# Weight splits held back while row maxima are due, and stages of the attention shifted, in a kernel whose instruction order is written out by a planner

## The chip, the cores and the metric

The kernel runs on one core of one Trainium2 chip. The metric is the device time of one execution in microseconds (us). Before the change the median of three runs is 1079.9 us (1079.01 to 1081.43).

## The reference, cut to what matters

One input X (2048 positions, width 640, fp32) goes through two blocks whose results are mixed by a gate.

```python
q, k, v = x @ wq, x @ wk, x @ wv          # 32 heads of 20, 4 segments of 512 positions
for s in range(4):
    p = softmax(qs @ ks.T * scale + mask)  # causal, inside the segment
    a_dot = p @ vs
    a_mem = (phi(qs) @ M) / (phi(qs) @ z + 1e-6)   # memory of the segments before
    o_s = g_h * a_mem + (1 - g_h) * a_dot
    M, z = M + phi(ks).T @ vs, z + sum(phi(ks))
a = o @ wo
b = (silu(x @ w1) * (x @ w3)) @ w2         # SwiGLU, inner width 1728
out = gate * a + (1 - gate) * b            # gate = sigmoid(sum(x * gate_w))
```

## The kernel before, in words

Every large matmul works on weights and activations that are split into a high and a low part, in three passes, and on halves of 64 rows, so that two matmuls can run side by side in TensorE (PE). A weight tile is loaded by a DMA (line 494), its high part is cast on ACT (line 181), and its low part is a subtraction on POOL (line 176, tile W). Letters in the profile are tiles: q, k, v, g, u, f and op are products with weights; s are logits, t transposed logits, P their exponentials, o the product of P with V; nd, gm, gd, gt and rr belong to the memory term and to the division by the row sums.

The attention runs over 64 pairs of heads (16 pairs for each of the 4 segments), and two pairs make a quad. For a pair, `s_unit` makes logits in three parts (s..._0 to s..._2) and DVE takes the row maxima from PSUM (line 1161, a custom instruction and a read of its result). `max_rows` splits the maxima of a quad, `turn` transposes them on DVE (line 1187), and `row_in` sends them by four small DMAs of POOL's queue (line 1171, qk<-mr, two for each pair) into two more rows of the pair's tile of q and k. `t_unit` then makes the transposed logits with the maximum already subtracted; its matmuls (line 1212) wait for these DMAs. ACT exponentiates (line 1219), POOL masks (line 1228), and `pv_quad` multiplies with V (line 1245). `load_pair` fetches q and k of a pair with two DMAs of 240 KB in the same POOL queue (line 1126, qk<-qkd). At the end of a segment, `o_sums` reads the row sums back, `o_scale` inverts them on DVE (line 1309) and scales them (line 1310).

The order on every engine is written out in Python. The planner keeps a clock for each engine and walks through slots: 40 slots (n) for a quad (m). The tables S_AT and T_AT put the units into slots, `after(k, f)` files f into the list `soon`, and `tick` counts k down by one at every slot. Between the units, steps of the other jobs are laid in at a fixed spacing: `w_step` runs once every STEP = 700 ns of planned time and splits the oldest loaded weight tile when its age allows it, and `braid(a, b, every, skip)` puts steps of job b between those of job a at a spacing `every` (ns of planned time) after a lead of `skip`. Each engine takes its instructions strictly in the order written, so one that waits holds everything behind it on that engine. PSUM has eight banks, handed out in turn: a matmul into a bank waits until the reader of the bank's last contents is done.

Of the kernel before, what the change touches and what calls it, by code (L numbers as in the profile page):

```python
# [21 lines left out]
S, D, H, DH, NSEG, L = 2048, 640, 32, 20, 4, 512  # L22
# [19 lines left out]
COL, COL4, MIN_MM, APART, ISSUE, AHEAD = 0.4533, 1.7, 62, 5, 580, 500  # L42
STEP, READ = 700, 222
EVAC = 1500
LAND, SPARE, NOP = 4200, 99999, 80
ENGINES = ("PE", "SP", "Activation", "DVE", "Pool")

# [2 lines left out]
def gated_mix(ctx: ExitStack, tc: tile.TileContext, xT, wqk, wv, w13, w2, w2h, wo, beta, out):  # L50
# [71 lines left out]
    def here(ins):  # L122
        return ins
# [9 lines left out]
    def now():  # L133
        return max(clocks)
# [315 lines left out]
    def room(tag, n=1):  # L450
        return sum(t <= now() for t in rings[tag]) >= n
# [8 lines left out]
    def big_tile(name, dt=F32):  # L460
        return sp.tile([P, KB * L], dt, tag="big", name=name, bufs=1)
# [16 lines left out]
    def limit():  # L478
        return NW + clock["oldest"] - sum(h < clock["oldest"] for s in floors.values() for h in s)

    early, raws, clock = [], [], dict(slot=0, step=0, oldest=0, next=0, raws=2)
# [33 lines left out]
    def w_step():  # L515

        clock["step"] += 1
        if raws and raws[0][0] in EARLY:
            if clock["step"] >= 6 + 2 * raws[0][0]:
                w_split()  # L520
        elif raws and raws[0][0] < limit() and now() >= raws[0][3]:
            w_split()
        use = clock["raws"] - NRAW
        if clock["next"] < min(len(items), limit() + NRAW) and \
                (use < 0 or use < len(freed) and now() >= freed[use]):
            w_load()
# [90 lines left out]
    def load_raw(c):  # L617

        wide = big_tile(f"xr{c}")
        xraw[c] = [wide[:, kb * L:(kb + 1) * L] for kb in range(KB)]  # L620
        for kb in range(KB):
            store_later(xraw[c][kb], xT[c, :, kb, :], ("x", c, kb))
        return
        yield
# [326 lines left out]
    def job_read(c):  # L951
        return 5.6, memory_read(c)
# [101 lines left out]
    def ffn_down(cs, js, idx, last=False, free=None):  # L1054
        first = js[0] == 0
        def tile_of(c, lb, hf):
# [18 lines left out]
            def evac(ps, bank):  # L1075
                dst = accs[c][:, lb, 320 * hf:320 * hf + 320]
                if first:
                    until[bank] = go("act", 530)
                    nc.scalar.activation(dst, ps[:, :320], AF.Copy, scale=cgate[:, c, lb:lb + 1])
                elif NF in js and busy["dve"] > max(busy["act"], now()) + EVAC and busy["pool"] < now() + 600 and room("f", 3):  # L1080
                    name = f"fe{c}_{lb}_{hf}"
# [33 lines left out]
    oall, heads, pairs = {}, {}, {}  # L1115
# [60 lines left out]
    def max_rows(p):  # L1176

        flush(lambda: all(f is not s_unit or q > p + 1 for _, f, q, _ in units))
        while min(pairs[p + k].get("rows", 0) for k in range(2)) < 6:
            force()  # L1180
        m = pairs[p]["m"]
        ns = nsT[p // 2 % 2]

        def turn():
            mr = sp.tile([32, P], F32, tag="mr", name="mr", bufs=1)
            for g in range(4):
                nc.vector.transpose(mr[:, 32 * g:32 * g + 32], ns[32 * g:32 * g + 32].bitcast(F32))
            go("dve", 840)
            for k in range(2):
                for a in range(2):  # L1190
                    dst = pairs[p + k]["t"][RH + a:RH + a + 65:64, 0].rearrange("h (b n) -> h b n", n=P)
                    r = 16 * a + 8 * k
                    after(3 + 6 * k + a, row_in, pairs[p + k], dst, mr[r:r + 8])

        split_psum(ns.rearrange("p (a n) -> p a n", a=2), m, f"nh{p}", turn, 200)

# [67 lines left out]
    def o_sums(c):  # L1264
        sums_of[c] = t = f_tile(f"rs{c}", "dve")
        here(nc.sync.dma_start(t[:, :P], od[c][:, DH].rearrange("h (a n) -> h a n", n=P)))
        go("sp", 600)
        after(9 if c < NSEG - 1 else 5, o_scale, c)
        after(4 if c < NSEG - 1 else 2, o_load, c, KB - 1)

    def o_load(c, b):
# [106 lines left out]
    soon = []  # L1378

    def after(n, f, *a):  # L1380
        soon.append([n, f, a])
# [8 lines left out]
    NQUAD = NJ // 4  # L1390
# [15 lines left out]
    def attention():  # L1406


        for m in range(-1, NQUAD + 2):
            for n in range(40):  # L1410
                if m == -1 and n < 40 - LEAD:
                    continue
                clock["slot"] += 1
                if n == 3 and 0 <= m - 2 < NQUAD:
                    units.append((clock["slot"], pv_quad, 2 * m - 4, 0))
                if n in S_AT and 0 <= m < NQUAD:
                    i, x = S_AT[n]
                    units.append((clock["slot"], s_unit, 2 * m + i, x))
                if n in T_AT and 0 <= m - 1 < NQUAD:
                    i, x = T_AT[n]  # L1420
                    units.append((clock["slot"], t_unit, 2 * m - 2 + i, x))
                if n == 24 and 0 <= m < NQUAD:
                    after(9, max_rows, 2 * m)
                if n in ((22, 32) if m < 0 else (28, 39)) and m + 1 < NQUAD:
                    p = 2 * (m + 1) + (n > 28)
                    flush(lambda: all(q % NST != p % NST for _, _, q, _ in units))
                    load_pair(p)
                if units and (units[0][0] + 2 * LATE < clock["slot"]):
                    unit()
                tick()  # L1430
                yield m
# [113 lines left out]
    def down_with_out(cs, g, c, mid):  # L1545

        plan = plan_wo()
        floors["o", c] = held = set(plan)
        o1, o2 = oproj(c, plan, held)
        cost, f = job_down(cs, g)  # L1550

        def mix():
            yield from islice(o2, 4)
            yield from islice(f, mid)
            yield from o2
            yield from f

        return (3.5, o1), (17.8 + cost, mix())
# [19 lines left out]
    def job_down(cs, g, last=False):  # L1578
        return 2.384 * sum(3 if j < NF else 1.5 for j in GROUPS[g]), ffn_down(cs, GROUPS[g], plan_down(GROUPS[g]), last)

    def jobs_up(cs, g):
        return [job_up(cs, j) for j in GROUPS[g]]

    def jobs_group(cs, g):
        return [job_up(cs, j) for j in GROUPS[g]] + [job_down(cs, g)]
# [14 lines left out]
    def alternate(a, b):  # L1600

        def gen():
            for y in a[1]:
                yield y
                z = next(b[1], None)
                if z is not None:
                    yield z
            yield from b[1]
        return a[0] + b[0], gen()

    def take(a, n):
        return a[0] / 2, (y for _, y in zip(range(n), a[1]))

    def chain(jobs):
        return sum(c for c, _ in jobs), (y for _, g in jobs for y in g)

    def braid(a, b, every, skip=0, rest=True):

        def gen():
            side = Side(b[1], every, skip)  # L1620
            yield side
            yield from a[1]
            side.on = False
            if side.held is not None:
                yield side.held
            if rest:
                yield from b[1]
        return a[0] + b[0], gen()

    A, B = (0, 1), (2, 3)  # L1630
# [7 lines left out]
    k, warm = bank_tile("warm")  # L1638
    until[k] = 8000.0
    for n in range(9):  # L1640
# [5 lines left out]

    seg = job_q2(A, 3)
    g = jobs_group(A, 0)
    seg += [braid(chain(g[:3]), job_read(1), 3800, 11000)] + g[3:] + jobs_group(A, 1) + jobs_up(A, 2) + [job_down(A, 2)]
    segs.append((H + LAG + 3, seg))  # L1650
    u = jobs_up(A, 5)
    o1, ud = down_with_out(A, 5, 0, 3)
    seg = [braid(chain(u), o1, 1400, 4000), ud]
    u0, u1 = jobs_up_by_chunk(A, 6)
    xs = chain([(0, new_x(2)), (0, new_x(3))])
    d0, d1 = jobs_down_by_chunk(A, 6)
    out0 = (0, store(0))
    q2, v2 = chain(job_q2((2,), 0, {2: big_tile})), job_v((2,))[0]
    seg += [(0, load_raw(2))] + u0 + [braid(braid(chain(u1), xs, 2700, 3400, False), d0, 900, 1000, False)]
    seg += [braid(braid(chain([d0, take(q2, 2), d1, q2, v2]), out0, 700), xs, 3000, 4000)]  # L1660
    seg += jobs_k(B)
    segs.append((2 * H + 4, seg))
    seg = job_q((2,), 2)
    q = job_q2(B, 3, {3: slot}) + job_q2((3,), 0) + job_q((3,), 2)
    up = job_up(B, 0)
    r = job_read(2)
# [3 lines left out]
    o1, ud = down_with_out(B, 0, 1, 1)  # L1670
    seg = [braid(braid(chain(main), chain([r, job_read(3)]), 1800, 0), o1, 1500, 5000),
           braid(ud, (0, store(1)), 900), *jobs_up(B, 1), job_down(B, 1)]
    segs.append((3 * H + LAG + 4, seg))
    u = jobs_up(B, 2)
    o1, ud = down_with_out(B, 2, 2, 4)
    seg = [braid(chain(u), o1, 1800, 2000), ud, *jobs_up(B, 3)]
    d = job_down(B, 3)
    seg.append(take(d, 7))
    segs.append((NJ + LAG + 0, seg))
    u = [job_up(B, j) for j in GROUPS[4]]  # L1680
    d2, d3 = jobs_down_by_chunk(B, 4)
    o1, o2 = jobs_oproj(3)
    tail = [braid(chain([d] + u + [d2, take(d3, 6)]), o1, 1100, 7000), alternate(take(o2, 3), take(d3, 0)), o2, d3]

    def at_job(n):
        if n == 0:
# [24 lines left out]
    while run:  # L1711
# [10 lines left out]
        while credit > 0:  # L1722
            d = step(run[1])
# [59 lines left out]
```

## Time and profile before

| | |
|---|---|
| median of 3 runs | 1079.9 us |
| profiled execution | 1081.12 us |
| its span on the core | 1079.3 us |
| granted TensorE clock | 1.000 of full speed |
| PE busy / weight loads (PEld) busy | 1072.3 us (99%) / 974.8 us (90%) |
| DVE / ACT / POOL busy | 577.7 / 490.4 / 572.0 us |
| chain that ended last | PE 96%, DMA 2%, POOL 1% |

The span is what the profiler sees between the first and the last instruction; the 1.8 us around it belong to start and end. Busy time of the engines other than PE matters only where PE waits for them. In the timeline a row is a run of like instructions (x2 is two of them), and the words in brackets give the idle time of that engine just before the row and what ended it.

### The profile page before, as it was taken

How to read it: one execution, taken by the hardware profiler on the slowest of the kernel's cores; microseconds unless marked ns; L12 is line 12 of the kernel's file. 1: busy time of each engine (PE TensorE's matmuls, PEld its weight loads, DVE VectorE, ACT ScalarE, POOL GpSimd, SP SyncE). 2: the span in 40 equal slices, each digit the busy share in tenths (PEclk: the TensorE clock that was granted, in tenths of full speed). 3: DMA queues.
4: the chain of work that ended last, by engine and by line, in shares of the span. 5: the costliest groups of instructions: out<-in, count | busy, mean ns of one | idle time of the engine just before them, and what ended most of it. 6: DMA issues, size and time to landing. Idle time of an engine off the chain costs nothing.

```text
span 1079.3 us, 29722 instructions
## 1 busy us (share of the span) xinstructions
PE 1072.3 (99%) x11681; PEld 974.8 (90%) x11681; DVE 577.7 (54%) x1740; ACT 490.4 (45%) x1015; POOL 572.0 (53%) x767
## 2 busy tenths in 40 slices
PE   9999999999999999999999999999999999999998
PEld 7999998978888999999988889999989889988998
DVE  6022565355545666656444766763446665553464
ACT  6255434644344344365656654445442444344221
POOL 3543456376366463546665556655554774574341
PEclk9999999999999999999999999999999999999999
DMA  9365754344353332528587876454444453442231
GB/s 323 129 207 193 265 142 124 77 109 113 80 133 105 101 88 68 172 68 260 162 279 221 281 230 196 138 148 113 129 116 99 124 141 78 105 130 66 62 99 74
DMA packets 88099, 154.98 MB, mean 144 GB/s; under 512 B 19628, under 2 KB 34904, under 8 KB 87960
## 3 DMA queue, kind: packets, MB, share of 16 engines
q1 hardware_dynamic: 56520, 96.88, 28.7%
q0 software_dynamic: 23664, 42.04, 15.9%
q10 hardware_dynamic: 7776, 14.16, 3.6%
q8 instruction: 93, 1.52, 0.6%
q14 instruction: 46, 0.38, 0.1%
HBM read 97.55 MB, written 54.53 MB: 141 GB/s over the span
## 4 chain that ended last, share of the span: by engine, by line
PE 96%; DMA 2%; POOL 1%; issue 0%; ACT 0%; SPq 0%; DVE 0%; POOLq 0%
PE g L266 19%; PE f L266 17%; PE u L266 17%; PE op L266 7%; PE v L266 7%; PE o L1245 6%; PE k L266 6%; PE q L266 4%; PE t L1212 4%; PE s L1150 4%; DMA qk<-mr 1%; PE pm L266 1%; PE q L778 1%; PE nd L266 1%; PE pkt L264 0%
## 5 line engine op out<-in xcount | busy, mean ns | idle before, releaser
L266 PE MATMUL g<-X,W 64*128 64x512 f32 x1680 | 398.9, 396 | 0.0
L266 PE MATMUL u<-X,W 64*128 64x512 f32 x1560 | 375.2, 394 | 0.0
L1161 DVE CUSTOM_DVE_ANT_0 junk<-s,mask 128x128 bf16<-128x128 f32 (+3 forms) x512 | 250.9, 490 | 165.4 <-PE s L1150 127.6
L266 PEld LDWEIGHTS g<-X,W 64*128 64x128 f32 x1680 | 276.6, 185 | 12.7 <-issue 1.8
L176 POOL TENSOR_TENSOR W<-wr,W 128x640 fp32r<-128x640 f32 (+1 forms) x132 | 206.6, 1572 | 145.2 <-ACT W L181 135.2
L266 PE MATMUL f<-W,ht 64*128 64x320 f32 x2592 | 276.1, 308 | 0.0
L266 PEld LDWEIGHTS u<-X,W 64*128 64x128 f32 x1560 | 259.5, 185 | 12.1 <-issue 1.2
L266 PEld LDWEIGHTS f<-W,ht 64*128 64x128 f32 x2592 | 260.5, 185 | 2.4 <-issue 1.6
L1219 ACT ACTIVATE P<-t 128x384 f32<-128x384 f32 (+1 forms) x384 | 180.4, 525 | 174.1 <-PE t L1212 158.4
L1228 POOL TENSOR_SCALAR_AFFINE_SELECT P<-P 128x256 f32<-128x256 f32 (+1 forms) x192 | 93.4, 495 | 172.3 <-ACT P L1219 165.0
L181 ACT CAST W<-wr 128x640 fp32r<-128x640 f32 (+1 forms) x138 | 98.4, 727 | 34.1 <-PE f L266 15.7
L266 PE MATMUL op<-W,oT 64*128 64x320 f32 x960 | 103.9, 307 | 0.0
L266 PEld LDWEIGHTS op<-W,oT 64*128 64x128 f32 x960 | 98.9, 185 | 0.9 <-issue 0.6
L266 PE MATMUL k<-X,W 64*128 64x512 f32 x600 | 98.2, 400 | 0.0
L1212 PE MATMUL t<-qk 62*128 62x256 f32 (+2 forms) x512 | 95.0, 326 | 1.7 <-DMA qk<-mr 1.7
L1026 POOL TENSOR_TENSOR ht<-ft,ht 128x512 fp32r<-128x512 f32 x52 | 67.2, 1293 | 52.3 <-ACT ht L1033 47.6
L1095 DVE SCALAR_TENSOR_TENSOR acc<-f,cgate,acc 128x320 f32<-128x320 f32 x124 | 66.6, 547 | 49.2 <-PE f L266 46.9
L1150 PE MATMUL s<-qk 60*128 60x256 f32 (+2 forms) x512 | 92.2, 325 | 0.0
L266 PE MATMUL v<-W,X 64*128 64x322 f32 (+2 forms) x948 | 90.6, 310 | 0.0
L1126 POOL DMA_DIRECT2D qk<-qkd x128 | 69.6, 548 | 35.1 <-PE f L266 29.9
L266 PEld LDWEIGHTS v<-W,X 64*128 64x128 f32 (+1 forms) x948 | 86.3, 186 | 0.3 <-ACT phi_qs L706 0.2
L266 PE MATMUL q<-X,W 64*128 64x512 f32 x480 | 83.7, 396 | 0.0
(121 smaller groups left out, 1312.4 us busy)
## 6 DMA issues: line engine op xcount, KB each, us to landing
qk<-qkd POOLq DMA_DIRECT2D x128, 240.0 KB, 4.2
wr<-in_w_dram SPq DMA_DIRECT2D x80, 320.0 KB
qkd<-qs SPq DMA_DIRECT2D x20, 512.0 KB
qkd<-ks SPq DMA_DIRECT2D x20, 512.0 KB
od<-oq ACTq DMA_DIRECT2D x32, 256.0 KB
wr<-in_wo_dram SPq DMA_DIRECT2D x20, 320.0 KB
vg<-vd SPq DMA_DIRECT2D x16, 336.0 KB
qkd<-qs SPq DMA_DIRECT2D x20, 256.0 KB
```

Source lines behind the costliest of these rows:

```text
L176: return lambda: e.tensor_sub(dst[:, 1], src, dst[:, 0].bitcast(F32))
L181: stages(bank, ("act", ns, lambda: nc.scalar.copy(dst[:, 0], src)), low, done=done)
L266: ins = nc.tensor.matmul(o, l, x, start=i == 0 and (r == 0 or not w.todo[0]), stop=i == len(todo) - 1 and (r == 1 or not w.todo[1]), skip_ ...
L1026: nc.gpsimd.tensor_sub(ht[:, 1], t, ht[:, 0].bitcast(F32))
L1095: nc.vector.scalar_tensor_tensor(dst, ps[:, :320], cgate[:, c, lb:lb + 1], dst, op0=ALU.mult, op1=ALU.add)
L1126: here(nc.gpsimd.dma_start(t[64 * i:64 * i + RH], qkd[c][RH * (h + i):RH * (h + i + 1)]))
L1150: nc.tensor.matmul(ps[i][:, o:o + n], q[:, qb * P:(qb + 1) * P], k[:, :n], start=qb != 1, stop=qb != 0, skip_group_check=True)
L1161: nc.vector.tensor_tensor_reduce(out=junk[:, :n], in0=ps[i][:, o:o + n], in1=mask[:, L - n:], scale=1.0, scalar=-3.0e38, op0=ALU.add, op1= ...
L1212: nc.tensor.matmul(ps[i][:, o:o + L - q0], k[:, kb * P:(kb + 1) * P], q[:, q0:], start=kb != 2, stop=kb != 3, skip_group_check=True)
L1219: nc.scalar.activation(u["P"][:, i, o:o + n], ps[i][:, b:b + n], AF.Exp, scale=SCALE)
L1228: nc.gpsimd.affine_select(d, d, pattern=[[0, 2], [0, n], [1, P]], base=0, channel_multiplier=-1, compare_op=ALU.is_ge, fill=0.0)
L1245: nc.tensor.matmul(ps[32 * i:32 * i + 32, kb * P:], heads[2 * p + i]["v"][:, kb], pairs[p + i // 2]["P"][:, i % 2, o:o + n], start=kb == 0 ...
```

## The change: what it does

A constant HOLD = 4 is added. `w_step` no longer begins to split a weight tile while a `row_in` stands in `soon` with fewer than 4 slots to go; the first tiles (EARLY) are not held. The `row_in` of a quad's second pair move from 9 and 10 slots after the transposition to 11 and 12. `o_scale` comes after 8 slots and not 9, in segments 0 to 2. `pv_quad` is filed at slot 2 of a quad and not at 3. Eight numbers in the lists of jobs change: six spacings and leads of `braid`, and two counts of steps (the last argument of `down_with_out`, and a `take`).

```diff
+HOLD = 4
...
-        elif raws and raws[0][0] < limit() and now() >= raws[0][3]:
+        elif raws and raws[0][0] < limit() and now() >= raws[0][3] and not any(f is row_in and n < HOLD for n, f, _ in soon):
             w_split()
...
-                    after(3 + 6 * k + a, row_in, pairs[p + k], dst, mr[r:r + 8])
+                    after(3 + 8 * k + a, row_in, pairs[p + k], dst, mr[r:r + 8])
...
-        after(9 if c < NSEG - 1 else 5, o_scale, c)
+        after(8 if c < NSEG - 1 else 5, o_scale, c)
...
-                if n == 3 and 0 <= m - 2 < NQUAD:
+                if n == 2 and 0 <= m - 2 < NQUAD:
                     units.append((clock["slot"], pv_quad, 2 * m - 4, 0))
...
-    seg += [braid(chain(g[:3]), job_read(1), 3800, 11000)] + g[3:] + jobs_group(A, 1) + jobs_up(A, 2) + [job_down(A, 2)]
+    seg += [braid(chain(g[:3]), job_read(1), 3600, 11000)] + g[3:] + jobs_group(A, 1) + jobs_up(A, 2) + [job_down(A, 2)]
...
-    tail = [braid(chain([d] + u + [d2, take(d3, 6)]), o1, 1100, 7000), alternate(take(o2, 3), take(d3, 0)), o2, d3]
+    tail = [braid(chain([d] + u + [d2, take(d3, 6)]), o1, 1100, 9000), alternate(take(o2, 2), take(d3, 0)), o2, d3]
```

The two programs hold the same instructions in the same numbers; only their order differs, and up to pair 16 the order on PE is the same. Line numbers of the changed kernel are higher by one. Three places follow, with the row after a kernel's name being the order on one engine.

First DVE, at the end of segment 0 (near 359 us of the trace before): the logits s19_1 of pair 19 and the inversion of the row sums rs0. Before:

```order
L1161 ISA junk_5610,m36_5217<-s19_1_0_5605,mask_85 128x384
L1161 ISA m36_5217 128x1
L1161 ISA junk_5612,m36_5217<-s19_1_1_5606,mask_85 128x384
L1161 ISA m36_5217 128x1
L1309 RECIPROCAL rs0_5521<-rs0_5521 128x128
L1095 SCALAR_TENSOR_TENSOR acc1_2960<-f1_6_0_0_5506,cgate_99,acc1_2960 128x320
```

and in the changed kernel:

```order
L1310 RECIPROCAL rs0_5514<-rs0_5514 128x128
L1162 ISA junk_5609,m36_5218<-s19_1_0_5604,mask_85 128x384
L1162 ISA m36_5218 128x1
L1162 ISA junk_5611,m36_5218<-s19_1_1_5605,mask_85 128x384
L1162 ISA m36_5218 128x1
L1096 SCALAR_TENSOR_TENSOR acc1_2960<-f1_6_0_0_5510,cgate_99,acc1_2960 128x320
```

The inversion (RECIPROCAL rs0) has moved ahead of the two row maxima (ISA junk, each with the read of its result) of s19_1, behind which it stood.

Second ACT, in segment 2 (near 666 us): t37 are transposed logits of pair 37, v3_2_1 is a product for V of segment 3, vv3_2_1 its copy in SBUF, vd3 the store of it. Before:

```order
L1219 ACTIVATE P37_10700<-t37_1_0_10770 128x384 [waits PE_49]
L1219 ACTIVATE P37_10700<-t37_1_1_10771 128x384 [waits PE_49]
L860 COPY vv3_2_1_10795<-v3_2_1_10606 128x16x20 [waits DMAHW7_49,PE_49]
L866 ACTIVATE gate_98<-v3_2_1_10606 128x1
L1219 ACTIVATE P37_10700<-t37_2_0_10809 128x384 [waits PE_49]
L1219 ACTIVATE P37_10700<-t37_2_1_10810 128x384 [waits PE_49]
L688 DMA vd3_75<-vv3_2_1_10795 128x336 [waits Activation_49,Pool_49]
```

and in the changed kernel:

```order
L861 COPY vv3_2_1_10797<-v3_2_1_10603 128x16x20 [waits DMAHW5_49,DMAHW1_49,PE_49]
L867 ACTIVATE gate_98<-v3_2_1_10603 128x1
L1220 ACTIVATE P37_10701<-t37_1_0_10802 128x384 [waits PE_49]
L1220 ACTIVATE P37_10701<-t37_1_1_10803 128x384 [waits PE_49]
L689 DMA vd3_75<-vv3_2_1_10797 128x336 [waits DMAHW4_49,Activation_49,Pool_49]
L1220 ACTIVATE P37_10701<-t37_2_0_10826 128x384 [waits PE_49]
L1220 ACTIVATE P37_10701<-t37_2_1_10827 128x384 [waits PE_49]
```

The copy vv3_2_1 and the small activation behind it (gate) have moved ahead of the exponentials of t37_1, and the copy now waits for two other DMA semaphores (DMAHW5 and DMAHW1) than before (DMAHW7).

Third PE, some 18 us later (near 685 us): s41_0 are logits of pair 41, g3_1, u2_1 and u3_1 products of the SwiGLU block. Before:

```order
L266 MATMUL g3_1_11046<-X3_7809,W86_10092 128x512
L266 MATMUL u3_1_11099<-X3_7809,W87_10313 128x512
L266 MATMUL g3_1_11046<-X3_7809,W86_10092 128x512
L1150 MATMUL s41_0_0_11133<-qk1_87 128x256 [waits DMASW6_49,DVE_49]
L1150 MATMUL s41_0_1_11134<-qk1_87 128x256 [waits DMASW7_49,Activation_49]
L1150 MATMUL s41_0_0_11133<-qk1_87 128x256
L1150 MATMUL s41_0_1_11134<-qk1_87 128x256
```

and in the changed kernel:

```order
L267 MATMUL u2_1_10923<-X2_7354,W87_10304 128x512
L1151 MATMUL s41_0_0_11104<-qk1_87 128x256 [waits DMASW5_49,DVE_49]
L1151 MATMUL s41_0_1_11105<-qk1_87 128x256 [waits DMASW6_49,Activation_49]
L1151 MATMUL s41_0_0_11104<-qk1_87 128x256
L1151 MATMUL s41_0_1_11105<-qk1_87 128x256
L267 MATMUL u3_1_11110<-X3_7809,W87_10304 128x512 [waits Activation_49]
```

Before, s41_0 comes after ten matmuls of u3_1; now it comes ahead of the first of them, and this first one has a wait for ACT of its own. t38_1, which stands a few rows above, has moved ahead by 24 matmuls of g3_1, u2_1 and u3_1, s41_0 by 20. On ACT the exponentials of t38_1 stand, in both programs, behind four casts of oT1 and the activation ft2_1.

## Rows read from the trace of the kernel before

**Rows 1.** Waits of PE, longest first: total us, times, longest.
```profile
PE t L1212 <- DMA qk<-mr: 1.7, 2, 1.4
PE warm L1641 <- DVE zero L1637: 1.3, 1, 1.3
```

**Rows 2.** Chain that ended last, in order of time: start us, us, what.
```profile
560.17 8.19 DMA qk<-mr
...
619.49 5.16 DMA qk<-mr
```

**Rows 3.** Timeline, POOL and PE near 560: start, us, work, idle before, releaser.
```profile
559.15 1.03 POOL L1126 DMA_DIRECT2D qk<-qkd  x2
...
561.70 1.56 POOL L176 TENSOR_TENSOR W<-wr,W 128x640 fp32r<-128x640 f32 x1 [0.95 <-ACT W L181]
...
568.50 0.68 PE L1212 MATMUL t<-qk 62*128 62x512 f32 x2 [1.42 <-DMA qk<-mr]
```

**Rows 4.** Windows: stretch, length, busy of PE, PEld, DVE, ACT, POOL, clock, DMA share, GB/s.
```profile
560.00:564.00 4.00, 4.00 (x37) 2.74 (x38) 2.82 (x10) 1.76 (x4) 2.98 (x5) 1.00 0.98 338
564.00:568.00 4.00, 3.08 (x42) 1.78 (x34) 0.50 (x1) 1.71 (x3) 1.61 (x4) 1.00 0.65 170
640.00:644.00 4.00, 4.00 (x57) 4.00 (x55) 1.95 (x7) 1.31 (x3) 3.98 (x8) 1.00 0.22 65
```

**Rows 5.** Timeline, DVE and PE near 359.
```profile
358.87 0.56 DVE L1161 CUSTOM_DVE_ANT_0 junk<-s,mask 128x384 bf16<-128x384 f32 x1
...
359.36 0.95 DVE L1309 RECIPROCAL rs<-rs 128x128 f32<-128x128 f32 x1
...
359.67 0.42 PE L1212 MATMUL t<-qk 62*128 62x256 f32 x4
```

**Rows 6.** Timeline, SP, ACT and PE near 666.
```profile
664.19 0.33 SPq L688 DMA_DIRECT2D gd<-gm  x1
...
666.59 0.43 ACT L860 COPY vv<-v 128x320 f32<-128x320 f32 x1 [0.21 <-PE v L266]
666.91 0.18 ACT L866 ACTIVATE gate<-v 128x1 f32<-128x1 f32 x1
...
666.75 0.49 PE L1212 MATMUL t<-qk 62*128 62x256 f32 x4
```

**Rows 7.** Tile gd: its stores, issue to landing.
```profile
DMA to landing us min/median/max: 3.3/3.9/6.0
```

**Rows 8.** Timeline, PE, DVE and ACT between 676 and 686.
```profile
676.73 0.40 PE L264 MATMUL gt<-ident,gm 64*128 64x64 f32 x4
...
677.32 0.68 DVE L1352 TENSOR_TENSOR oall<-oall,gt 128x512 f32<-128x512 f32 x1
...
678.93 0.56 DVE L1161 CUSTOM_DVE_ANT_0 junk<-s,mask 128x384 bf16<-128x384 f32 x1
...
678.03 1.24 ACT L181 CAST oT<-oall 128x384 fp32r<-128x384 f32 x3 [0.23 <-DVE oall L1352]
680.15 0.60 ACT L999 ACTIVATE ft<-g 128x512 f32<-128x512 f32 x1 [0.88 <-PE g L266]
...
684.86 0.87 ACT L1219 ACTIVATE P<-t 128x384 f32<-128x384 f32 x2 [3.49 <-PE t L1212]
...
685.60 0.49 PE L1150 MATMUL s<-qk 60*128 60x256 f32 x4
```

**Rows 9.** Chain that ended last, ten 64x512 matmuls in a row.
```profile
691.53 1.16 PE u L266 x10
```

**Rows 10.** Timeline, DVE and POOL near 674.
```profile
673.59 3.40 DVE L875 TENSOR_SCALAR gate<-gate 128x4 f32<-128x4 f32 x1
...
671.72 3.08 POOL L176 TENSOR_TENSOR W<-wr,W 128x640 fp32r<-128x640 f32 x2
...
675.39 1.57 POOL L176 TENSOR_TENSOR W<-wr,W 128x640 fp32r<-128x640 f32 x1
```

**Rows 11.** Line 875 on DVE: count, ns min/median/max.
```profile
L875 DVE TENSOR_SCALAR gate<-gate x4: 260/292/3401, 41.2 to 673.6; 128x4 f32<-128x4 f32 x4
```

More of the change, by code (lines that the diff above doesn't have):

```diff
@@ L1648, in gated_mix @@
     g = jobs_group(A, 0)
-    seg += [braid(chain(g[:3]), job_read(1), 3800, 11000)] + g[3:] + jobs_group(A, 1) + jobs_up(A, 2) + [job_down(A, 2)]
+    seg += [braid(chain(g[:3]), job_read(1), 3600, 11000)] + g[3:] + jobs_group(A, 1) + jobs_up(A, 2) + [job_down(A, 2)]
     segs.append((H + LAG + 3, seg))
     u = jobs_up(A, 5)
-    o1, ud = down_with_out(A, 5, 0, 3)
-    seg = [braid(chain(u), o1, 1400, 4000), ud]
+    o1, ud = down_with_out(A, 5, 0, 4)
+    seg = [braid(chain(u), o1, 1400, 4500), ud]
     u0, u1 = jobs_up_by_chunk(A, 6)
@@ L1658, in gated_mix @@
     q2, v2 = chain(job_q2((2,), 0, {2: big_tile})), job_v((2,))[0]
-    seg += [(0, load_raw(2))] + u0 + [braid(braid(chain(u1), xs, 2700, 3400, False), d0, 900, 1000, False)]
-    seg += [braid(braid(chain([d0, take(q2, 2), d1, q2, v2]), out0, 700), xs, 3000, 4000)]
+    seg += [(0, load_raw(2))] + u0 + [braid(braid(chain(u1), xs, 3000, 1800, False), d0, 900, 1000, False)]
+    seg += [braid(braid(chain([d0, take(q2, 2), d1, q2, v2]), out0, 700), xs, 3000, 7000)]
     seg += jobs_k(B)
```

## The prediction

> **What bounds the kernel now.** I read the page's busy shares first: PE works 99% of the span, at the full granted clock, so only time in which PE waits, or matmuls that pack better, can be won. Next came the waits of PE. There the reader is to see two groups alone: the transposed logits t wait for the small transfers of row maxima, 1.7 us in all in two places, and the start waits 1.3 us for its first operand, which the change leaves [rows 1]. No group names a weight tile: no wait for a split is on record. Then the chain that ended last: it leaves PE for two transfers of row maxima, 8.19 us and 5.16 us long [rows 2].
>
> The timeline around the longer one shows who is ahead of whom. POOL issues two loads of a pair (240 KB each) at 559.15, the row transfer at 560.17, and begins the weight split at 561.70, behind the transfer; t starts at 568.50 after 1.42 us of idle PE [rows 3]. The windows give the reason: the DMA engines are 0.98 busy in the four microseconds in which the transfer sets out, while in a quiet stretch they are 0.22 busy [rows 4]. So what held the row maxima here was other traffic, not a weight split. The second place (619.49) has the same pattern.
>
> **The change, part by part.** The sum is made against the profiled execution, 1081.1 us, which lies 1.2 us above the median.
>
> *Held splits.* A split is a cast on ACT and 1.56 us on POOL [rows 3]; holding one moves it back by a few slots. PE never waits for a weight tile in the trace, so I cost the hold at nothing; what covers it is the stock of split tiles, and if that were too short in one place, the price is a split, 1.6 us. As for its gain: at the two places where t waits, the row transfers, the pair loads and the split stand on POOL in the same order in both programs, with the split already behind. The stall stays; four small transpositions (pkt) now stand ahead of the first waiting t and fill some of it: −0.2 us. Bounds: −1.7 (both waits gone) and 0.
>
> *Row transfers of the second pair later.* By the tables the first pair of a quad has nine slots from its transfer to its t (slot 36 to slot 45), and the second had 25 and now has 23. Both recorded waits are of first pairs, with nine slots; a second pair with over twice as many costs 0. At pair 36 a load of a pair has slipped ahead of the second of the first pair's transfers; the DMA engines are nearly idle there, 0.22 [rows 4], so 0, and a miss would cost no more than the longest wait on record, 1.42 us.
>
> *The inversion of row sums one slot earlier.* RECIPROCAL, 0.95 us, now stands ahead of two row maxima of 0.56 us each with their reads. Before, the second maximum ends at about 359.4 (start 358.87), and the next t, which needs the banks that the maxima read, starts at 359.67 [rows 5]. The inversion delays the second maximum to about 360.3; with two more matmuls ahead of it t is due at 359.8: +0.45 us. Bounds: 0 (its row sums arrive late, or the bank is another) and 0.95. In the other segments no row maximum changes sides with it.
>
> *The copy ahead of the exponentials.* The change lets the copy vv3_2_1 pass the exponentials of pair 37 on ACT. The tile that it writes was read last by a store of gd. That store is issued at 664.19 before [rows 6]; nine matmuls fewer stand ahead of its data, so about 663.5 now, and such stores take 3.3 to 6.0 us to land, 3.9 at the median [rows 7]: 667.4. Copy and gate take 0.43 and 0.18 us [rows 6]; they free the bank for t37_2 at 668.0. t37_2 ran at 666.75 [rows 6] and has eight small matmuls (some 0.6 us) more ahead: due at 667.35. That is +0.65 us; by the ends of the landing times 0 and 2.7.
>
> *Logits of pair 41 earlier.* s41_0 and the u3_1 behind it need the banks that the exponentials of t38_1 empty, and these stand on ACT behind the oT casts and ft2_1. PE's side moves ahead: 20 matmuls of 0.116 us [rows 9] are 2.3 us, so s41_0 is due at 683.3 (685.60 before). ACT's side moves back: the transposition gt1_2 has 11 large and some ten small matmuls more ahead and ends near 679.3 (676.73 plus 0.4, and 2.2). On DVE its evacuation now stands behind the row maxima that end at 679.5 before [rows 8] and some 0.5 later now: 680.0, plus 0.68, four casts at 0.41, ft at 0.60 and two exponentials, 0.87 together [rows 8], make 683.5 for the first bank and 683.9 for the second. Both ends move together when PE slips earlier. Cost: 0.2 for s41_0 and 0.3 for u3_1, +0.5 us. Bounds: 0 and 3.6 (the second rival adds 3.1).
>
> *pv_quad a slot earlier, and the spacings.* One slot less for the masks of the exponentials: PE has no recorded wait for a mask [rows 1], so 0. The spacings move steps of memory, store and SwiGLU work; what that does at named places is in the terms above, the rest is 0 with half a microsecond either way.
>
> Sum: −0.2 + 0.45 + 0.65 + 0.5 = +1.4 us, 1082.5 on the profiled execution's basis, and 1081.3 on the median's.
>
> **A rule against the trace.** In the trace a DVE instruction on 128x4 numbers takes 3.40 us at 673.59, while the other three of its line lie near 0.26 to 0.29; POOL's splits run from 671.72 to 674.80 and from 675.39 to 676.96, and DVE is released as the last one ends [rows 10, 11]. The Trainium skill, "SBUF — State Buffer", section "Who interferes with whom", says that VectorE in a two-port mode and GpSimd contend for one shared pair of ports, and that the one that comes second blocks fully until the other is done. The trace agrees: 3.40 us. By this rule a split that is held back is no delay saved but a block moved to other DVE work, which makes the second rival.
>
> **The rivals.**
> *Faster: the waits for row maxima go.* If the new spacing thins the traffic ahead of the two transfers, 1.7 us goes [rows 1] and the three new waits do not come: 1079.9 − 1.7 = 1078.2. To pass the bound of 0.2% (2.16 us, about what can be told from no change here) another 0.5 us must come from better packing of matmuls. For it: 8.19 us for 4 KB leaves much to win. Against it: the order of POOL's queue is unchanged there.
>
> *Slower: splits block DVE ahead of pair 41.* In the changed order the gate instruction stands ahead of the evacuations of gt1_4 and gt1_2 (before, of gt1_2 alone, and nothing on PE waited), and two splits run back to back on POOL near it. If it meets them at their start, DVE is held 3.40 − 0.29 = 3.1 us, gt1_2's evacuation, the casts, the exponentials and s41_0 all slip, and the time is 1081.3 + 3.1 = 1084.4. It costs from the point at which DVE is held for more than nothing, since that chain has no reserve left. Against it: the third split, which prolonged the block before, is now behind the row transfers, so the gate may find POOL between splits.
>
> *Slower: the store lands late.* With 6.0 us instead of 3.9 [rows 7], t37_2 waits 2.7 instead of 0.65: 1081.3 + 2.1 = 1083.4. For it: the pair loads and V's stores share the queues there. Against it: the median.
>
> *Nothing comes through.* The stores land at 3.3 us, the evacuations have a few tenths more than I count: 1079.9, with the row waits as before.
>
> **How the numbers follow.** The sum, +0.7 to +2.1 us: 0.33, and it is the likeliest, 1081.3. Nothing comes through: 0.25. Row waits gone and better packing: 0.13. DVE blocked: 0.14. Store late: 0.15. The 0.2% bounds around the median are 1077.7 and 1082.1; the first two cases lie inside: 0.58. The faster rival, with its packing, gives 0.13, the two slower ones 0.29. The range leaves out one in ten on each side: 1077.7 (row waits and half a microsecond of packing) to 1084.5 (DVE blocked). The forecast's own range is 1080.5 to 1082.1.
>
> **What would show it.** Right: in the waits of PE, t on row maxima still near 1.5 us, and new small waits of t on DVE near 360 us, of t on ACT near 667 and of s and u on ACT near 683; the copy vv in front of the exponentials with idle ACT before it. The gate instruction of line 876 at 0.3 us or at 3 tells the second rival. Wrong: row transfers near 560 and 619 that land in 3 us, or PE's waits no longer than before with the time changed all the same, which would mean that the matmuls themselves pack differently.

## The result: about 2 us slower, and the profile after

The changed kernel takes 1081.24 us (median of 22 runs, 1079.91 to 1081.69), the kernel before 1079.26 us (22 runs, 1078.19 to 1081.43). The ratio is 1.0015, 95% interval [1.0009, 1.0021]: a loss of 1.6 us by this ratio and of 2.0 us by the medians. It is below the 0.2% that the prediction took as no change, but the interval does not hold 1. The profiled execution of the changed kernel has a span of 1079.9 us.

The waits of PE in the changed kernel (columns as in [rows 1], of which these are the counterpart):

```profile
PE warm L1642 <- DVE zero L1638: 1.3, 1, 1.3
PE nd L267 <- SPq L270: 0.5, 1, 0.5
PE t L1213 <- ACT gate L867: 0.5, 1, 0.5
PE k L267 <- SPq L270: 0.4, 1, 0.4
PE s L1151 <- DMA qk<-qkd: 0.2, 1, 0.2
PE t L1213 <- DVE m L1162: 0.2, 1, 0.2
```

The 1.7 us of t on row maxima [rows 1] are gone, and several small waits stand in their place. Two of them were forecast by name: t on DVE and t on ACT. That of nd on SP is no mark of the change: a second profile of the kernel before has it too (below). One caution goes for all of them: this view counts only time in which both halves of PE stand still. Where one half waits and the other works on alone, the loss is larger, and is read from the starts in the timeline.

The first place, DVE and PE near 360 us, the counterpart of [rows 5]:

```profile
358.81 0.94 DVE L1310 RECIPROCAL rs<-rs 128x128 f32<-128x128 f32 x1
359.67 0.49 DVE L1162 CUSTOM_DVE_ANT_0 junk<-s,mask 128x384 bf16<-128x384 f32 x1
...
360.32 0.56 DVE L1162 CUSTOM_DVE_ANT_0 junk<-s,mask 128x384 bf16<-128x384 f32 x1
...
360.48 0.28 PE L1213 MATMUL t<-qk 62*128 62x256 f32 x1
360.94 0.50 PE L1213 MATMUL t<-qk 62*128 62x256 f32 x3 [0.18 <-DVE m L1162]
```

The inversion now runs first, the second row maximum begins at 360.32, and the second half of the logits t16_2 has to wait for it. From the first matmul's start to the last one's end it is 0.96 us (360.48 to 361.44), where the same four took 0.42 [rows 5].

The second place, ACT and PE near 666 us, the counterpart of [rows 6]:

```profile
666.58 0.43 ACT L861 COPY vv<-v 128x320 f32<-128x320 f32 x1 [3.28 <-DMA gd<-gm]
666.91 0.18 ACT L867 ACTIVATE gate<-v 128x1 f32<-128x1 f32 x1
...
666.37 0.28 PE L1213 MATMUL t<-qk 62*128 62x256 f32 x1
667.13 0.50 PE L1213 MATMUL t<-qk 62*128 62x256 f32 x3 [0.48 <-ACT gate L867]
```

ACT stands idle for 3.28 us ahead of the copy vv, which waits for the store of gd; before, the copy waited 0.21 us, for PE. In the chain that ended last (start, us, what) this store has taken the place of the row maxima of [rows 2]:

```profile
662.18 4.34 DMA gd<-gm
...
930.90 5.39 DMA qk<-qkd
```

The other transfer on it, a pair load, costs s the 0.2 us of the list above.

t37_2 runs from 666.37 to 667.63, 1.26 us where it took 0.49 [rows 6]: 0.77 us.

The third place, DVE, ACT and PE between 680 and 684 us, the counterpart of [rows 8]:

```profile
680.42 0.68 DVE L1353 TENSOR_TENSOR oall<-oall,gt 128x512 f32<-128x512 f32 x1
...
681.14 1.24 ACT L182 CAST oT<-oall 128x384 fp32r<-128x384 f32 x3 [2.66 <-DVE oall L1353]
682.28 0.58 ACT L1000 ACTIVATE ft<-g 128x512 f32<-128x512 f32 x1
682.77 0.86 ACT L1220 ACTIVATE P<-t 128x384 f32<-128x384 f32 x2
...
682.65 0.39 PE L267 MATMUL g<-X,W 64*128 64x512 f32 x1
682.88 0.92 PE L1151 MATMUL s<-qk 60*128 60x256 f32 x4
683.68 1.19 PE L267 MATMUL u<-X,W 64*128 64x512 f32 x8
```

ACT waits 2.66 us for the evacuation of gt1_2, then runs casts, ft and exponentials in one unbroken row, and s41_0 takes 0.92 us in place of 0.49 [rows 8]: its second half waits for the first of the two exponentials, and u3_1 at 683.68 for the second, which ends at 683.63.

The same in windows (columns as in [rows 4]); first the kernel before in the last place, then the changed one near 560, 666 and 682:

```profile
680.00:684.00 4.00, 4.00 (x40) 4.00 (x38) 3.73 (x12) 1.21 (x2) 2.00 (x1) 1.00 0.67 205
```

```profile
560.00:564.00 4.00, 4.00 (x43) 2.95 (x43) 2.56 (x9) 2.31 (x5) 3.00 (x5) 1.00 0.94 328
...
664.00:668.00 4.00, 3.52 (x46) 3.13 (x45) 2.31 (x9) 1.42 (x5) 0.95 (x3) 1.00 0.83 261
680.00:684.00 4.00, 3.86 (x33) 3.18 (x31) 3.61 (x11) 2.86 (x7) 0.00 (x0) 1.00 0.49 130
```

In 680 to 684 PE is idle for 0.14 us only, but it starts 33 matmuls instead of 40. The two windows do not hold the same matmuls, so the columns are the better measure: by the matmuls that start inside, 16720 before and 13568 now. The difference, 3152 columns, is that of 6.2 matmuls of 512, and at 0.116 us each [rows 9] it is worth 0.7 us, most of it lost by one half alone.

Last, POOL and PE near 560, the counterpart of [rows 3]:

```profile
559.65 1.03 POOL L1127 DMA_DIRECT2D qk<-qkd  x2
560.67 0.58 POOL L1172 DMA_DIRECT2D qk<-mr  x1
562.25 1.55 POOL L177 TENSOR_TENSOR W<-wr,W 128x640 fp32r<-128x640 f32 x1 [1.00 <-ACT W L182]
...
567.44 0.45 PE L1213 MATMUL t<-qk 62*128 62x512 f32 x2
```

The order on POOL and the DMA load (0.94 busy, 0.98 before [rows 4]) are as before, yet t at 567.44 waits for nothing: the transfer landed after 6.18 us, not 8.19 [rows 2]. Whether the change did that is a question for the experiments.

### The profile page after: what moved, and what is told of

Its sections match the earlier page's. It is cut to its first block, busy times and chain, and to the rows that moved or that the text cites. A ratio compares the mean times of both kernels' runs of the same rounds, so it can differ in the third digit from the quotient of the medians.

```text
span 1079.9 us, 29731 instructions
## 1 busy us (share of the span) xinstructions
PE 1073.0 (99%) x11681; PEld 975.5 (90%) x11681; DVE 576.0 (53%) x1740; ACT 489.2 (45%) x1015; POOL 572.6 (53%) x767
## 4 chain that ended last, share of the span: by engine, by line
PE 97%; DVE 1%; DMA 1%; ACT 0%; issue 0%; SPq 0%; POOL 0%; ACTq 0%; DVEq 0%
PE g L267 19%; PE u L267 18%; PE f L267 17%; PE op L267 7%; PE o L1246 7%; PE v L267 7%; PE k L267 6%; PE q L267 5%; PE s L1151 4%; PE t L1213 4%; PE q L779 1%; PE pm L267 1%; PE nd L267 1%; DMA qk<-qkd 0%; PE pkt L265 0%; PE gt L265 0%
```

## The experiments

The theory: the loss is the sum of the three new waits, at t16_2, t37_2 and s41_0 with u3_1. The rivals: it is the hold itself, or matmuls that pack differently; and, for the waits that went, that the hold or the later transfers removed them.

**Three edits of the changed kernel, each taking one wait away, and all three at once.** These ran on one chip, beside 33 runs of the kernel before (median 1079.76).

The inversion of segment 0 in two halves, the second behind the row maxima:

```diff
-        stages(None, ("dve", 950, lambda: nc.vector.reciprocal(rs, rs)),
+            n = 64 if c == 0 else P
+            nc.vector.reciprocal(rs[:, :n], rs[:, :n])
...
+            if c == 0:
+                nc.vector.reciprocal(rs[:, 64:], rs[:, 64:])
```

> The changed kernel, with one edit: in segment 0 the inversion of the row sums is done in two halves of 64 columns, the first where the whole one stood, the second behind the two row maxima of pair 19; every other instruction stays where it was. Theory of the three waits (the sum of the prediction): the maxima end some 0.4 us earlier, the wait of t16_2 near 360 us (0.43 us in the changed kernel's trace) falls to 0.1 or less, and the time falls by 0.4 us, from 1.0015 to about 1.0011 of the kernel before. Rival (the waits are covered: PE loses nothing by them, and the time comes from matmuls that pack differently): the wait goes, the time stays at 1.0015.

Measured: 1080.89 us, 1.0011 [1.0002, 1.0020]. In its profile the wait of t on DVE is gone; that of t on ACT is 0.7 us, where the changed kernel has 0.5.

The store that the copy vv waited for, reading another tile:

```diff
-                store_later(gd[c][:, qb, 320 * hf:320 * hf + 320], gm, ("g", c, qb, hf), t=t, done=lambda: let(name))
+                src = Xs[2][:, 0, 0, :320].bitcast(F32) if (c, qb, hf) == (2, 3, 1) else gm
+                store_later(gd[c][:, qb, 320 * hf:320 * hf + 320], src, ("g", c, qb, hf), t=t, done=lambda: let(name))
```

> The changed kernel, with one edit: one store of the memory term of segment 2 (gm2_3_1, 160 KB) takes its bytes from the tile X, with the same size, queue and place, so the ring tile is not read by it (this block of the result is left out, so the output is not the reference's). The copy vv3_2_1 on ACT no longer waits for that store to land. Theory of the three waits: t37_2 near 667 us no longer waits (0.81 us in the changed kernel's trace); the time falls by 0.8 us, from 1.0015 to 1.0008. Rival (another buffer or engine is as late, the wait is given back within the next 20 us): the wait of t37_2 goes, those of s41_0 and u3_1 grow by as much, the time stays at 1.0015.

Measured: 1080.44 us, 1.0007 [0.9999, 1.0016]. The wait of t on ACT is gone, and s41_0 still takes 0.92 us: what was won at t37_2 is not given back there. In this one profile t waits 0.6 us for row maxima in another place.

Two of the four oT casts of one block on POOL instead of ACT:

```diff
-        stages(bank, ("act", ns, lambda: nc.scalar.copy(dst[:, 0], src)), low, done=done)
+        stages(bank, ("act", ns, lambda: (cast or nc.scalar.copy)(dst[:, 0], src)), low, done=done)
...
+                  cast=nc.gpsimd.tensor_copy if c == 1 and qb == 1 else None)
```

> The changed kernel, with one edit: two of the four casts of oT1 (0.41 us each) go from ACT to POOL, at the same place of the program; ACT reaches ft2_1 and the exponentials of t38_1 some 0.8 us earlier. Theory of the three waits: s41_0 and u3_1 near 683 us wait 0.60 and 0.55 us in the changed kernel; now 0 and 0.3 at most; the time falls by 0.8 us, from 1.0015 to 1.0008. Rival (DVE's evacuation of gt1_2 or PE itself sets the end there, or POOL is late): waits as before, time at 1.0015.

Measured: 1080.51 us, 1.0007 [0.9998, 1.0016]. s41_0 takes 0.61 us (683.03 to 683.64) in place of 0.92, and u3_1 starts beside it, at 683.32.

All three edits together:

> The edits of the three kernels before together on the changed kernel (one block of the memory result is left out, as there). Theory of the three waits: 0.4 + 0.8 + 0.8 = 2.0 us less than the changed kernel, some 1079.2 us, a ratio of 0.9997 to the kernel before (0.9990 to 1.0004). Rival (packing of matmuls makes the difference, waits are covered): 1.0015 as the changed kernel. A mixture (part is given back): between 1.0004 and 1.0012.

Measured: 1079.65 us, 0.9996 [0.9987, 1.0005]. Its waits of PE hold none of the three:

```profile
PE warm L1652 <- DVE zero L1648: 1.3, 1, 1.3
PE q L779 <- ACT X L576: 1.0, 1, 1.0
PE t L1214 <- DMA qk<-mr: 0.3, 1, 0.3
PE s L1152 <- DMA qk<-qkd: 0.2, 1, 0.2
```

What follows: against the 1.0015 of the changed kernel the single edits give 0.0004, 0.0008 and 0.0008. None is told apart from it alone, since the intervals overlap. Together they give 0.0019, that is 2.1 us, and here the intervals [0.9987, 1.0005] and [1.0009, 1.0021] are apart. So the loss lies in these three waits, and a difference in packing is not needed for it. That they add up one by one is what the middle values say, not more. One rival was not tried: the three edits in the kernel before, where they might win time without any of these waits.

**The stall at 560.** Is it the traffic of the pair loads, and does it come every time? First the kernel before with the loads of pairs 33 and 37 cut from 512 columns to 8, so that almost nothing of them is moved:

```diff
-            here(nc.gpsimd.dma_start(t[64 * i:64 * i + RH], qkd[c][RH * (h + i):RH * (h + i + 1)]))
+            n = 8 if p in (33, 37) else L
+            here(nc.gpsimd.dma_start(t[64 * i:64 * i + RH, :, :n], qkd[c][RH * (h + i):RH * (h + i + 1), :, :n]))
```

> The kernel before, with one edit: the loads of pairs 33 and 37, which POOL issues just ahead of the two row transfers that t waited for, move 8 of 512 columns (the rest of these two pairs is left out, so the output is not the reference's); no instruction moves. Theory (other traffic, these loads first, holds the row transfers): the transfer at 560 us, 8.19 us before, lands in 3 to 4.5 us, t waits for no row maxima, and the time falls by what the waits cost in a usual run, 0.5 to 1.7 us: ratio 0.9984 to 0.9995. Rival (the 8.19 us of the one profile were the exception, and the transfer usually lands just in time): it lands earlier too, but the time stays within 0.03%: 0.9997 to 1.0003.

Measured: 1078.67 us beside 1079.43 (21 runs) for the kernel before, 0.9993 [0.9984, 1.0002]. t waits for no row maxima in its profile, and the transfer near 560 lands after 4.04 us, as the theory said, where in all other profiles here it takes 5.4 to 8.2. So the pair loads do hold the row transfers. As to time it is inconclusive, since the interval holds 1.

Then the kernel before once more, without an edit:

> The kernel before unchanged, for a second profile. Theory (its order makes the wait of t on row maxima): the transfer near 560 us takes 7.5 us or more, t waits 1 us or more again. Rival (it varies from run to run): 5.5 to 7 us as in the changed kernel and its variants (6.18, 5.59, 6.71, 6.05, 6.40 us), and a wait of 0.3 us at most.

The two longest waits of PE in that second profile of the kernel before, beside that for the first operand; only one of 0.2 us, of k on SP, is left out:

```profile
PE q L778 <- ACT X L575: 1.3, 1, 1.3
...
PE nd L266 <- SPq L269: 0.6, 1, 0.6
...
```

and its timeline, POOL and PE near 560, then SP and PE near 617:

```profile
561.52 0.58 POOL L1171 DMA_DIRECT2D qk<-mr  x1
...
568.16 0.59 PE L1212 MATMUL t<-qk 62*128 62x512 f32 x2
...
615.93 2.37 SPq L688 DMA_DIRECT2D gd<-gm  x1
...
618.41 0.34 PE L266 MATMUL nd<-Ms,pq 64*128 64x84 f32 x1 [0.64 <-SPq L269]
```

The same program, and no wait of t for row maxima: the transfer at 561.52 landed within 6.64 us, where it took 8.19 in the first profile. Other waits are there: that of q comes at the start, near 11 us, and that of nd is for a no-op of SP that is queued behind a store whose issue alone took 2.37 us. So the kernel does not make the largest wait of the first profile in every execution, and its absence in one profile of the changed kernel can't be put down to the change.

The row transfers of the first pair one slot earlier, in the kernel before:

```diff
-                    after(3 + 6 * k + a, row_in, pairs[p + k], dst, mr[r:r + 8])
+                    after(2 + 6 * k + a, row_in, pairs[p + k], dst, mr[r:r + 8])
```

> The kernel before, with one edit: all row transfers leave one slot earlier (2 + 6 k + a slots after the transposition, not 3 + 6 k + a), with nothing held and nothing else moved on purpose. Theory (first pairs' transfers are the late ones, and their own slot decides): t's waits on row maxima go wherever they were and the time falls by 0.5 to 1.7 us: 0.9984 to 0.9995. Rival (those waits are rare): 0.9997 to 1.0003.

Measured: 1080.19 us, 1.0009 [1.0000, 1.0017]. A miss: no gain, rather a small loss. In its profile t waits for nothing near 560 and 620, as the theory had it (and as in the second profile of before), and 0.3 us for row maxima in one other place, near 941; the time did not fall.

The store with the long issue, moved from SP's queue to ACT's, in the kernel before:

```diff
-            queue.dma_start(dst, src)
+            (nc.scalar if key == ("g", 2, 0, 0) else queue).dma_start(dst, src)
```

> The kernel before, with one edit: the first store of the memory term of segment 2 (gm2_0_0, near 616 us) is issued by ACT's queue, not by SP's, where its issue takes 1.84 to 2.37 us in every profile so far while PE (nd2_0_1) waits for SP behind it, 0.5 to 1.06 us. Theory (SP is held by the issue, ACT's ring has room): the wait of PE for SP near 617 us goes and the time falls by 0.5 to 1.0 us: 0.9990 to 0.9996. Rival (the issue takes as long on ACT, and what stands behind it there waits): 1.0000 to 1.0010.

Measured: 1080.10 us beside 1079.56 (22 runs), 1.0003 [0.9995, 1.0012]. The timeline of ACT and PE:

```profile
616.58 0.33 ACTq L688 DMA_DIRECT2D gd<-gm  x1
...
624.02 0.59 PE L1212 MATMUL t<-qk 62*128 62x512 f32 x2 [1.09 <-DMA qk<-mr]
```

On ACT's queue the issue takes 0.33 us, and nd no longer waits. But t now waits 1.09 us for row maxima six microseconds on, at a place where it waited 0.32 us in the first profile of before and for nothing in the second. From 616 to 624 us the share of the DMA engines is 1.00 and more here, and a wait that is taken away at one place comes back at the next. The other profiles show the same exchange. Apart from the hold alone there are twelve: in eight of them nd waits 0.35 to 0.64 us for SP near 617 and t waits for nothing near 623, in four (the first one of before, the other tile, all three edits, and this one) t waits 0.32 to 1.09 us and nd does not, and in none both wait. So the expectation's "every profile so far" was too wide; with the other tile and with all three edits the issue on SP took only 1.24 and 1.13 us. That both waits come from one limit is my reading of these profiles; the time says only that nothing was gained.

**The parts of the change.** The hold alone, in the kernel before:

```diff
+HOLD = 4
...
-        elif raws and raws[0][0] < limit() and now() >= raws[0][3]:
+        elif raws and raws[0][0] < limit() and now() >= raws[0][3] and not any(f is row_in and n < HOLD for n, f, _ in soon):
```

> The kernel before with HOLD alone (no weight tile begun while a row transfer is due within four slots; no stage and no spacing changed). Theory of the prediction (no wait of PE is caused by a split, so the hold has nothing to win, and what it moves can only add waits elsewhere): 1.0000 to 1.0030. Rival (splits ahead of row transfers cost t its waits): t waits for no row maxima, 0.9980 to 0.9995.

Measured: 1085.41 us (5 runs) beside 1079.43, 1.0048 [1.0035, 1.0060]: slower by more than either theory allowed. The timeline of POOL and PE near 620, in the kernel before:

```profile
618.33 0.58 POOL L1171 DMA_DIRECT2D qk<-mr  x1
618.90 0.59 POOL L1292 DMA_DIRECT2D rR<-rs  x1
619.49 0.54 POOL L1171 DMA_DIRECT2D qk<-mr  x1
...
624.89 0.59 PE L1212 MATMUL t<-qk 62*128 62x512 f32 x2 [0.32 <-DMA qk<-mr]
```

and with the hold alone:

```profile
617.62 0.57 POOL L1172 DMA_DIRECT2D qk<-mr  x1 [1.73 <-DVE m L1162]
618.21 1.58 POOL L177 TENSOR_TENSOR W<-wr,W 128x642 fp32r<-128x642 f32 x1
619.73 0.57 POOL L1172 DMA_DIRECT2D qk<-mr  x1
...
624.55 0.59 PE L1213 MATMUL t<-qk 62*128 62x512 f32 x2 [1.82 <-DMA qk<-mr]
```

Count back from the time at which PE was ready for t: 624.57 before (624.89 − 0.32) and 622.73 with the hold. Before, the two transfers set out 6.24 and 5.08 us ahead of it, with the hold 5.11 and 3.00. A rule meant to keep splits away from the transfers has put one, 1.58 us, between them, where before the issue of one small load (rR) stood, 0.59 us: it holds only the beginning of a split, and what it holds back moves everything behind it. This is about half of the lost lead of 2.08 us: the two transfers are 2.11 us apart in place of 1.16. The other 1.13 us were lost ahead of the first one, for which POOL waits 1.73 us on the row maxima m. The 1.82 us of idle PE then cost more than themselves. In windows of that kernel:

```profile
623.00:624.00 1.00, 0.00 (x0) 0.00 (x0) 0.00 (x0) 0.00 (x0) 0.00 (x0) 1.00 1.07 401
...
626.00:627.00 1.00, 1.00 (x9) 1.00 (x7) 0.59 (x4) 0.82 (x2) 0.52 (x2) 0.50 0.57 103
```

After the idle stretch the granted clock stands at 0.50, the lower level of 1.2 GHz, and PE starts 9 matmuls in a microsecond. The three runs of this kernel with a mean clock of 0.998 took 1085.41 to 1085.57 us, the two with 1.000 took 1082.67 and 1083.93. If the drop is what tells the three from the two (it is seen in the one profile, of 1085.57 us), it is worth 1.5 to 2.9 us where it comes. It is not the whole loss: the two runs without it are still 3.2 and 4.5 us behind 1079.43. The profile has more waits that the first one of before lacks, of s on a pair load (0.6 us), of nd on ACT (0.6) and of q on SP (0.4); what each costs was not tried.

The changed kernel without the hold, the reverse of that diff's last line:

> The changed kernel without HOLD (splits begin as before); the shifted stages and spacings stay. Theory (the three waits come from the shifted stages, not from the hold): t16_2 near 360 us and t37_2 near 667 us wait as in the changed kernel (0.43 and 0.5 to 1.0 us), logits of pair 41 wait near 683 us in some part; 1.0010 to 1.0022. Rival (the hold, which alone costs 0.48%, carries the loss here too): 0.9995 to 1.0005 and no such waits.

Measured: 1081.39 us beside 1079.56, 1.0017 [1.0008, 1.0026], as with the hold (1.0015). Its profile has the waits of t on DVE and on ACT, 0.2 us each, and one of s on ACT's exponentials, 0.5. So inside the change the hold does not carry the loss, and no gain by it can be told either: between the ends of the two intervals (1.0008 to 1.0026 and 1.0009 to 1.0021) lie at most 1.8 us.

Two stage shifts alone, in the kernel before:

```diff
-        after(9 if c < NSEG - 1 else 5, o_scale, c)
+        after(8 if c < NSEG - 1 else 5, o_scale, c)
...
-                if n == 3 and 0 <= m - 2 < NQUAD:
+                if n == 2 and 0 <= m - 2 < NQUAD:
```

> The kernel before with two edits of the change alone: pv_quad at slot 2, o_scale after 8. Theory (these two bring the waits): t16_2 near 360 us waits 0.4 us, t37_2 near 667 us 0.5 to 1.0 us, logits of pair 41 near 683 us 0.5 to 1.5 us; 1.0012 to 1.0025. Rival (the spacings of braid or the row transfers of second pairs bring them): no such waits, 0.9995 to 1.0005.

Measured: 1082.62 us (6 runs) beside 1079.56, 1.0032 [1.0020, 1.0044]. The new waits are all there (the last three of its list):

```profile
...
PE s L1150 <- ACT P L1219: 0.5, 1, 0.5
PE t L1212 <- ACT gate L866: 0.2, 1, 0.2
PE t L1212 <- DVE m L1161: 0.2, 1, 0.2
```

These two lines of the diff bring the waits by themselves; which of the two brings which was not tried. By the middle values they cost more than the whole change, and the rest of it (later transfers, spacings) wins back 1.0032 − 1.0015, 1.8 us. The intervals touch at 1.0020 to 1.0021, so that is likely and not shown. Nor was it traced what their loss of some 3 us holds beyond the 2 us of the three waits.

## Why the prediction was right in time, and where its steps were not

**The time.** Forecast 1081.3, measured 1081.24, a loss of 1.6 to 2.0 us by ratio or medians where the sum said 1.4. That the figure agrees to 0.1 us is luck in part: it stands on 1079.9, the median of three runs, and 22 runs of the kernel before give 1079.26, so that a start 0.6 us too high made up for a loss 0.6 us too small (by the medians). The three waits came to 2.0 us by the timeline (0.54, 0.77 and 0.7) and 2.1 by the experiment, where I put 1.6. The rest of the change, by the middle value of the kernel without the three waits, took 0.4 off, which is not told from nothing, where I put −0.2 for another reason.

**Row maxima (forecast −0.2 us, "the stall stays").** The step failed, though its price was small. The split stands behind the transfer in the changed kernel's profile too, as read from the order. That other traffic holds these transfers, as I read from the windows, is borne out by the small loads (4.04 us). But the prediction took the 8.19 us of one execution as the kernel's, and a second profile of the same program has no such wait. What the waits for row maxima cost on the mean of many executions is not known; the small loads, at 0.9993 [0.9984, 1.0002], allow anything between 1.7 us and nothing.

**The inversion (forecast 0.45).** The step held: 0.54 longer in the timeline, 0.0004 of the time when half of it was moved back, which is 0.43 us, but not told from nothing by itself. Its name was not exact: o_scale is filed from pv_quad, and both came a slot earlier, so the inversion came two slots earlier.

**The copy behind the store (forecast 0.65).** The mechanism held, and the delay is 0.77 us, but the instants did not: the store sets out at 662.18 instead of the 663.5 that I put, takes 4.34 us instead of 3.9 and lands at 666.52 instead of 667.4, and t37_2 is due at 666.37 instead of 667.35. Both ends came some 0.9 us earlier than I put them, and these errors cancelled. With the store reading another tile the time falls by 0.0008, 0.9 us at the middle value.

**s41_0 and u3_1 (forecast 0.5).** The mechanism was right and the term too small: 0.7 us by the columns, 0.0008 (0.9 us) by the experiment. The prediction had the banks free at 683.5 and 683.9 (its own terms add up to 683.4 and 683.8); the trace has the two exponentials from 682.77 to 683.63, some 0.3 earlier. But PE was there earlier still: the last product ahead of s41_0 starts at 682.65, so that s41_0 was due 0.116 later [rows 9], at 682.77 and not at 683.3. The reserve between the two was half a microsecond smaller on PE's side and three tenths better on ACT's, and the difference came twice, at s41_0 and at u3_1.

**The hold (forecast 0).** Inside the change this held, as far as the runs can tell. As a rule for other uses it did not: alone it costs 0.0048, and the cover that I named, the stock of split tiles, was not what failed. The order of other work was.

**The gate under POOL's splits (a rival, forecast 3.1 us if it came).** It came in small. The timeline of DVE and POOL near 674, the counterpart of [rows 10, 11]:

```profile
674.09 0.79 DVE L876 TENSOR_SCALAR gate<-gate 128x4 f32<-128x4 f32 x1
...
677.35 0.69 DVE L1353 TENSOR_TENSOR oall<-oall,gt 128x512 f32<-128x512 f32 x1 [2.02 <-PE gt L265]
...
671.70 3.08 POOL L177 TENSOR_TENSOR W<-wr,W 128x640 fp32r<-128x640 f32 x2
```

Two splits run without a gap from 671.70 to 674.78, the gate meets them near their end, and it is held for 0.79 − 0.29 = 0.5 us until they are done. The rule of the Trainium skill, "SBUF — State Buffer", section "Who interferes with whom", that the second of the two engines blocks until the other is through, agrees with this. It does not by itself account for all of the 3.40 us before: there POOL was between splits from 674.80 to 675.39 [rows 10], issuing a row transfer, and DVE was held through that gap to the end of the third split; in the changed kernel it was free when the second split ended, with a row transfer issued behind it too. Why is open. The half microsecond reached nobody, since DVE then waits 2.02 us for PE. The prediction gave this chain no reserve, and here it had two microseconds: met at the start of the pair the gate would have been held 2.6 us longer, and by these rows some 0.6 us of it would have come through (an estimate), not 3.1.

**The other rivals.** The late store did not come: 4.34 us of the 3.3 to 6.0. "Nothing comes through" is refuted by the three waits in the profile. "Row waits gone and better packing" got its first half in one profile, by chance, and no gain.

**What stays open.** With the three waits gone the rest of the change is worth between −1.4 and +0.5 us (0.9987 to 1.0005). None of these kernels is shown to be faster than the one before.

## What to carry to other kernels

On a queue that works in order, an instruction moved ahead brings its own waits ahead of everything behind it: price the copy by who still reads the tile that it writes (when the store sets out, how long it lands), and subtract when PE is due. A wait for a small transfer among full DMA engines must be seen in a second profile of the same program before a gain is built on it. A time that comes out right can hide errors that cancel: check the instants of each link, not only the difference. A rule that keeps one kind of work away from another in a planned order needs a look at where the held work goes instead.

## What was not expected of the hardware

Two stretches of idle PE of like length ended differently: after 1.42 us at 568.50 [rows 3] the profile shows the clock at 1.00 on, after 1.82 us with the hold alone it fell to 0.50 for some three microseconds. The issue of one store took 2.37 us on SP's queue with the share of the DMA engines at 1.06, and 0.33 us on ACT's in another execution, 0.7 us later and with the share at 1.03. A 4 KB transfer landed in 1.6 us at the least, 2.8 to 2.9 at the median, and 8.2 or 6.5 at the most in two profiles of one program; near 560 us it took 4.04 us with the pair loads ahead of it cut to almost nothing.
